# The second mixture reads split rows of tokens from DRAM, with three more places for weight pairs

## The chip, the cores and the metric

One core of a Trainium2 chip runs one program: attention, a mixture of experts with hard routing, and a second mixture with soft weights. The metric is the device time of one execution in microseconds (us). The kernel before takes 2384.46 us, the median of three runs (2382.55 to 2384.86). TensorE (PE in the profile) multiplies, VectorE (DVE), ScalarE (ACT) and GpSimd (POOL) do elementwise work, and SyncE (SP) issues most DMAs, in the order of its program.

## The reference, cut to what matters

The second mixture, for 2304 tokens of width 512, eight experts and a hidden width of 1024:

```python
def _moe2_ref(x, w_gate, w1, w2):
    logits = x @ w_gate
    P = np.exp(logits - logits.max())
    for _ in range(8):
        P /= P.sum(1, keepdims=True) + 1e-09
        P /= P.sum(0, keepdims=True) + 1e-09
        P *= N / E
    out = np.zeros((N, D))
    for e in range(E):
        h = np.maximum(x @ w1[e], 0.0)
        out += P[:, e:e + 1] * (h @ w2[e])
```

Its x is the output of the first mixture, whose own x is the output of attention.

## The kernel before, in words

A float32 product is made of three matmuls: each operand is split into a high part (h at the end of its name: xh, w1h, w2h, hh) and the rest (xl, w1l, w2l, hl), and `mm3` (L842 and after) adds high times high, high times low and low times high. A split costs one copy on ScalarE, which makes the high part, and one subtraction on VectorE or GpSimd, which makes the low one.

The second mixture starts at about 765 us of the profiled execution. It runs over 8 experts, 9 blocks of 256 tokens and 4 steps each: 288 steps of 45 matmuls. In a step, `first` multiplies a block of x by a quarter of w1 (24 matmuls into the PSUM tile ph); then ScalarE makes z (with relu), VectorE four sums of its parts, ScalarE hh and VectorE hl. While that goes on TensorE makes the products of hh, hl of the step before with a quarter of w2 (`second`, 21 matmuls): seven products of Strassen's scheme in place of eight, which is why z has sums and w2 has sums too. `gather_up` adds the products from the PSUM banks (rows u, c) and adds them, times P, to acc.

x stands in SBUF as the tile xT2, unsplit. `split_x` splits a quarter of a block at a time, during the block ahead: two quarters with the subtraction on GpSimd, two on VectorE. Every block is split anew for every expert, 72 times.

The weights of an expert are four w1 pairs and four w2 pairs (a pair is a high and a low tile). They come as raw halves by DMA (`w_load`, 256 KB each, on SyncE), are split by `split`, and for w2 `strassen` also makes sums on GpSimd, in place in raw, between two stages of splits (a third tile, w3, holds two of the seven operands). There are four places for w1 pairs and four for w2 pairs, so the next expert's pair can only be made when the last block of this expert has used the place. `work(2)`, at the end of each step, puts up to two pieces of that into the engines' queues if a place is free. Around each of the seven changes of expert (a boundary below) the four w1 pairs and four w2 pairs of the next expert are made in some seven steps:

```python
if g >= gone[n] + 4 or budget < 1:
    continue
```

Each engine works strictly in the order of its program, which is written by hand from the first mixture on (`manual_schedule`): z and hl of a step stand on VectorE behind the weight splits that the step before put there. In the same way a DMA that waits on SyncE holds up those behind it.

In the first mixture (535 to 765 us) an expert has 288 tokens and 8 steps; xT2 is written at the end of each expert. In the last expert's steps 4 to 7 block 0 is split for the second mixture.

Of the kernel before, what the change touches and what calls it, by code (L numbers as in the profile page):

```python
# [9 lines left out]
F32 = mybir.dt.float32  # L10
# [5 lines left out]
OP = mybir.AluOpType  # L16
# [23 lines left out]
GBUSY = (10, 2, 4)  # L40
FAST = tuple(x.split() for x in (
# [25 lines left out]
def fused_kernel(ctx, tc, qT, kT, vv, wg1, w1a, w2a, wg2, w1b, w2b, out):  # L67
# [11 lines left out]


# [27 lines left out]
    def w_tiles(name, pool=None):  # L108
        pool, k = pool or wpool, {"w1": 4, "w2": 5, "w3": 2}[name]
        return [pool.tile([128, k, 256], F32R, name=name + x, tag=name + x, bufs=NFC // 2) for x in "hl"]  # L110
# [11 lines left out]
    def strassen(t, t2, b1, b2):  # L122
# [3 lines left out]
        seq = [lambda o=o, x=x, y=y: G.tensor_tensor(out=o, in0=x, in1=y, op=OP.subtract)  # L126
                for o, x, y in ((b11, b12, b11), (b12, b22, b12), (b22, b22, b11), (b21, b22, b21))]
# [711 lines left out]
    xT2 = x2.tile([128, NDC, N], F32, name="xT2")  # L839
# [9 lines left out]

    rw = ctx.enter_context(tc.tile_pool(name="rw", bufs=1))  # L850
# [22 lines left out]
    def work(budget):  # L873
# [46 lines left out]
    part1 = ctx.enter_context(ExitStack())  # L920
# [63 lines left out]
    pend, done, xa = None, 0, []  # L984
    for e in range(E):
        x, nxt = nxt, []
        for f in range(NFC):
# [17 lines left out]
            if e == E - 1 and f >= 4:  # L1005
                xa.append(split_x(0, f - 4, V))
# [53 lines left out]
    def first(w1, x, between):  # L1060
# [5 lines left out]
        between()  # L1066
# [4 lines left out]
        A.activation(z[:, :4], ph.rearrange("p f (t n) -> p (f t) n", t=2), AF.Relu)  # L1071
# [182 lines left out]
```

## Time and profile before

| | |
|---|---|
| median of 3 runs | 2384.46 us (2382.55 to 2384.86) |
| profiled execution | 2386.12 us |
| its span, first to last instruction | 2384.2 us |
| TensorE busy in the span | 2283.8 us, 96% |
| VectorE, ScalarE, GpSimd busy | 73%, 53%, 36% |
| granted TensorE clock, mean | 0.983 |
| DMA of SyncE's queue (q1) | 86.66 MB, 12.0% of 16 engines |
| xl on GpSimd, 144 rows | 137.1 us |

A matmul's own time in the profile (0.28 us for 256 columns) overlaps those of its neighbours, so the number of matmuls that pass in a stretch says more of TensorE than its busy time.

### The profile page before, as it was taken

What the parts mean: (1) busy time and instruction counts of PE and PEld (TensorE: products, weight loads), DVE (VectorE), ACT (ScalarE), POOL (GpSimd) and SP (SyncE); (2) the same over time, 40 slices, a digit from 0 to 9 for tenths busy, and PEclk for the clock granted to TensorE, in tenths of its full rate; (3) what the DMA queues carried; (4) which work ended last, traced back from release to release, by engine and by line L of the source; (5) the groups of instructions that cost most, each with busy time, mean ns of one, the idle gap of its engine ahead of it and who ended that gap; (6) DMA issues with size and microseconds to landing.
All of it is one profiled execution on the core that took longest, in us unless ns stands there. A gap on an engine that the chain in (4) does not pass through costs nothing.

```text
span 2384.2 us, 49700 instructions
## 1 busy us (share of the span) xinstructions
PE 2283.8 (96%) x19592; PEld 2158.1 (91%) x19592; DVE 1751.6 (73%) x4432; ACT 1269.8 (53%) x2805; POOL 851.3 (36%) x936
## 2 busy tenths in 40 slices
PE   9999999959999999999899999989999998998998
PEld 6888888729999999899899989989989998998998
DVE  8999999863444776866866786686687668668766
ACT  8999999614555434444444444454444444435443
POOL 6888888504445201400510330050041023005112
PEclk9999999859999999999999999999999999999999
DMA  2102010125554000200200010020010001001000
GB/s 79 56 29 64 26 57 15 36 79 150 169 167 134 28 1 10 63 1 1 63 10 1 28 45 1 1 72 1 1 54 19 1 19 54 1 1 45 23 23 36
DMA packets 54723, 99.36 MB, mean 42 GB/s; under 512 B 10832, under 2 KB 11088, under 8 KB 54480
## 3 DMA queue, kind: packets, MB, share of 16 engines
q1 hardware_dynamic: 51504, 86.66, 12.0%
q0 software_dynamic: 2976, 9.44, 1.1%
q8 instruction: 155, 2.54, 0.4%
q14 instruction: 88, 0.72, 0.1%
HBM read 86.63 MB, written 9.45 MB: 40 GB/s over the span
## 4 chain that ended last, share of the span: by engine, by line
PE 58%; issue 7%; DVE 6%; POOL 4%; ACT 2%; DMA 0%; POOLq 0%; DVEq 0%
PE bank L845 10%; PE bank L847 10%; PE bank L846 10%; PE ph L846 9%; PE ph L845 9%; PE ph L847 9%; POOL raw L126 2%; DVE w2l L115 1%; POOL w1l L115 1%; DVE z L1073 1%; ACT hh L1077 1%; DVE hl L1079 1%; POOL xl L959 1%; PE bank L949 1%; DVE z L1075 1%
## 5 line engine op out<-in xcount | busy, mean ns | idle before, releaser
L845 PE MATMUL ph<-xh,w1h 128*128 128x256 f32 x2304 | 647.2, 281 | 15.8 <-ACT z L1071 15.4
L846 PE MATMUL ph<-xl,w1h 128*128 128x256 f32 x2304 | 646.7, 281 | 9.3 <-DVE xl L959 9.3
L847 PE MATMUL ph<-xh,w1l 128*128 128x256 f32 x2304 | 643.9, 279 | 0.0
L959 POOL TENSOR_TENSOR xl<-xT,xh 128x256 fp32r<-128x256 f32 x144 | 137.1, 952 | 1056.6 <-ACT xh L957 1056.6
L845 PEld LDWEIGHTS ph<-xh,w1h 128*128 128x128 f32 x2304 | 433.3, 188 | 21.4 <-ACT z L1071 21.4
L1071 ACT ACTIVATE z<-ph 128x512 f32<-128x512 f32 x288 | 171.5, 595 | 513.3 <-PE ph L847 507.6
L846 PEld LDWEIGHTS ph<-xl,w1h 128*128 128x128 f32 x2304 | 432.5, 188 | 13.6 <-DVE xl L959 13.6
L847 PEld LDWEIGHTS ph<-xh,w1l 128*128 128x128 f32 x2304 | 432.7, 188 | 0.0
L847 PE MATMUL bank<-w2h,hl 128*128 128x256 f32 x1440 | 408.1, 283 | 14.4 <-DVE hl L1078 14.4
L845 PE MATMUL bank<-w2h,hh 128*128 128x256 f32 x1440 | 405.9, 282 | 10.1 <-ACT c L1099 10.1
L846 PE MATMUL bank<-w2l,hh 128*128 128x256 f32 x1440 | 403.0, 280 | 0.0
L1073 DVE TENSOR_TENSOR z<-z 128x128 f32<-128x128 f32 x288 | 104.3, 362 | 319.8 <-ACT z L1071 319.7
L1077 ACT ACTIVATE hh<-z 128x512 fp32r<-128x512 f32 x288 | 182.2, 633 | 275.0 <-DVE z L1076 275.0
L847 PEld LDWEIGHTS bank<-w2h,hl 128*128 128x128 f32 x1440 | 271.5, 189 | 18.8 <-DVE hl L1078 18.5
L845 PEld LDWEIGHTS bank<-w2h,hh 128*128 128x128 f32 x1440 | 271.0, 188 | 11.5 <-ACT c L1099 11.5
L846 PEld LDWEIGHTS bank<-w2l,hh 128*128 128x128 f32 x1440 | 271.4, 189 | 0.0
L1079 DVE TENSOR_TENSOR hl<-z,hh 128x512 fp32r<-128x512 f32 x288 | 204.4, 710 | 65.8 <-ACT hh L1077 65.8
L267 POOL TENSOR_TENSOR W<-W,sg 128x288 f32<-128x288 f32 x288 | 208.2, 733 | 69.8 <-ACT sg L262 69.2
L115 POOL TENSOR_TENSOR w1l<-raw,w1h 128x512 fp32r<-128x512 f32 x92 | 129.3, 1420 | 173.2 <-ACT w1h L114 147.1
L252 DVE MAX8 upper<-W 128x8 f32<-128x288 f32 x432 | 183.3, 448 | 5.7 <-POOL W L267 4.3
L334 PEld LDWEIGHTS pO<-vt,aT 128*128 128x128 f32 x1280 | 159.3, 193 | 28.2 <-issue 26.3
L291 POOL TENSOR_TENSOR dbuf<-S,upper 128x576 f32<-128x576 f32 x144 | 165.1, 1147 | 0.0
(238 smaller groups left out, 5402.8 us busy)
## 6 DMA issues: line engine op xcount, KB each, us to landing
raw<-in_w1a_dram SPq DMA_DIRECT2D x64, 256.0 KB, 2.9
raw<-in_w2a_dram SPq DMA_DIRECT2D x64, 256.0 KB, 2.8
raw<-in_w2b_dram SPq DMA_DIRECT2D x64, 256.0 KB, 2.7
raw<-in_w1b_dram SPq DMA_DIRECT2D x64, 256.0 KB, 2.6
vt<-in_vv_dram SPq DMA_DIRECT2D x16, 325.0 KB, 3.1
kt<-in_kT_dram SPq DMA_DIRECT2D x16, 288.0 KB, 3.4
qt<-in_qT_dram SPq DMA_DIRECT2D x16, 288.0 KB, 3.7
x_dram<-x SPq DMA_DIRECT2D x15, 256.0 KB, 2.7
```

The lines of the kernel that those rows point to most:

```text
L115: lambda: eng.tensor_tensor(out=t[1][:, s], in0=raw, in1=t[0][:, s], op=OP.subtract)]
L252: V.max(out=upper[:, ST[n]["at"], 8 * k:8 * k + 8], in_=ST[n]["W"])
L267: G.tensor_tensor(out=d["W"], in0=d["W"], in1=d["sg"], op=OP.mult)
L291: G.tensor_tensor(out=flat(d["D"])[:, :S], in0=flat(d["S"]), in1=upper[:, d["at"], 0:1].to_broadcast([128, S]), op=OP.subtract)
L334: PE.matmul(pO[:, 0], aT[:, c, :], vt[:, c, j], start=(c == 0), stop=(c == 4))
L845: PE.matmul(dst, a[0], b[0], start=start, stop=False, **kw)
L846: PE.matmul(dst, a[0], b[1], start=False, stop=False, **kw)
L847: PE.matmul(dst, a[1], b[0], start=False, stop=stop, **kw)
L959: eng.tensor_tensor(out=lo, in0=src, in1=hi, op=OP.subtract)
L1071: A.activation(z[:, :4], ph.rearrange("p f (t n) -> p (f t) n", t=2), AF.Relu)
L1077: A.activation(hh[:, 3:], z[:, 4:], AF.Copy)
L1079: V.tensor_tensor(out=hl[:, 3:], in0=z[:, 4:], in1=hh[:, 3:], op=OP.subtract)
```

## The change

The low and high parts of x are made once for each block and kept in DRAM. Blocks 0 to 6 are split at the ends of the first mixture's experts 1 to 7, as soon as their tokens are there; each is then written by two stores of 512 KB from SyncE (`split_x`). Blocks 7 and 8 are split in steps 0 and 1 of the second mixture. `load_x` reads a block back by two loads; blocks 0 and 1 are loaded at the end of the first mixture, and from then on the last step of each block issues the loads of the block after the next, into two buffers. xT2 is given up after step 3, acc takes room that it had, and after step 6 there are two further places for w1 pairs and one for w2 pairs, used from the second expert on. The sums of z are made in another order and with other signs, and so are those of w2.

```diff
+EXTRA = {"w1": 2, "w2": 1}
+    xp_dram = [[dram.tile([128, NDC * 256], F32, name=f"xp{x}{k}") for x in "hl"] for k in range(N // 256)]
-        seq = [lambda o=o, x=x, y=y: G.tensor_tensor(out=o, in0=x, in1=y, op=OP.subtract)
-                for o, x, y in ((b11, b12, b11), (b12, b22, b12), (b22, b22, b11), (b21, b22, b21))]
+        seq = [lambda o=o, x=x, y=y, op=op: G.tensor_tensor(out=o, in0=x, in1=y, op=op)
+                for o, x, y, op in ((b11, b12, b11, OP.subtract), (b12, b22, b12, OP.subtract),
+                                    (b22, b11, b22, OP.subtract), (b21, b21, b22, OP.add))]
...
+    def places(n, g):
+        return NFC // 2 + (EXTRA[n] if g >= 36 else 0)
+
     def make(n, g, raws):
-        W[n, g] = t = w_tiles(n)
+        at = (more[n], EXTRA[n]) if g >= 36 and (g - 36) % places(n, g) < EXTRA[n] else ()
+        W[n, g] = t = w_tiles(n, *at)
...
-            if g >= gone[n] + 4 or budget < 1:
+            if g >= gone[n] + places(n, g) or budget < 1 or g >= 36 and not more:
                 continue
...
-    def split_x(blk, d, eng):
+    def split_x(t, blk, d):
 
         src = xT2[:, d, blk * 256:(blk + 1) * 256]
-        hi = xs.tile([128, 256], F32R, name="xh", bufs=6)
-        A.activation(hi, src, AF.Copy)
-        lo = xs.tile([128, 256], F32R, name="xl", bufs=6)
-        eng.tensor_tensor(out=lo, in0=src, in1=hi, op=OP.subtract)
-        return hi, lo
+        A.activation(t[0][:, d], src, AF.Copy)
+        V.tensor_tensor(out=t[1][:, d], in0=src, in1=t[0][:, d], op=OP.subtract)
+        if d == NDC - 1:
+            for k in range(2):
+                nc.sync.dma_start(xp_dram[blk][k], all_of(t[k]).bitcast(F32))
+
+    def load_x(blk):
+        t = x_tiles(xs, 2)
+        for k in range(2):
+            nc.sync.dma_start(all_of(t[k]).bitcast(F32), xp_dram[blk][k])
+        return [(t[0][:, d], t[1][:, d]) for d in range(NDC)]
...
-            if e == E - 1 and f >= 4:
-                xa.append(split_x(0, f - 4, V))
+            if f >= 4 and (halved + (f > 4)) * 256 < e * CAP and (f > 4 or (halved + 1) * 256 <= e * CAP):
+                if f == 4:
+                    xt = x_tiles(xs, 2)
+                split_x(xt, halved, f - 4)
+                halved += f == NFC - 1
+            if e == E - 1 and f == NFC - 1:
+                xa = [load_x(0), load_x(1)]
...
-        V.tensor_tensor(out=z[:, 4], in0=z[:, 0], in1=z[:, 2], op=OP.add)
-        V.tensor_tensor(out=z[:, 6], in0=z[:, 1], in1=z[:, 0], op=OP.subtract)
-        V.tensor_tensor(out=z[:, 5], in0=z[:, 4], in1=z[:, 1], op=OP.subtract)
-        V.tensor_tensor(out=z[:, 7], in0=z[:, 3], in1=z[:, 5], op=OP.subtract)
+        sums(4, 2, 0, OP.add)
+        sums(5, 1, 4, OP.subtract)
+        sums(7, 3, 5, OP.add)
+        sums(6, 1, 0, OP.subtract)
...
-                both("u3", "u3", p4, OP.subtract, to=(t1, l)), *put("u3", t1, l), *scale(t1), *store(t1)]
+                both("u3", "u3", p4, to=(t1, l)), *put("u3", t1, l), *scale(t1), *store(t1)]
...
-            h = first(need("w1", 32 + 4 * e + i), x,
-                      lambda: xa.extend(split_x((blk + 1) % nb, d, V) for d in (2, 3)) if i == 3 else None)
+            h = first(need("w1", 32 + 4 * e + i), x)
+            if i == 3 and eb + 2 < E * nb:
+                xa.append(load_x((blk + 2) % nb))
...
-        if i == 1 or i == 2:
-            xa.append(split_x((blk + 1) % nb, i - 1, G))
+        if s < nb - halved:
+
+            xt = x_tiles(sx, 2)
+            for d in range(NDC):
+                split_x(xt, halved + s, d)
+        if s == 3:
+            turned.close()
+            ac = late["ac"] = ctx.enter_context(tc.tile_pool(name="ac", bufs=1))
+            late["acc"] = ac.tile([128, NT, D], F32, name="acc")
+        if s == 6:
+            more["w1"] = ctx.enter_context(tc.tile_pool(name="w1x", bufs=1))
+            more["w2"] = ctx.enter_context(tc.tile_pool(name="w2x", bufs=1))
```

VectorE's order at the change from the second to the third expert, last block, third step. Before: the second stage of one w2 pair (w2l, w3l), the first stage of the next (w2l, w2l), two rows of x, then the sums z and the two hl of the following step.

```order
L115 TENSOR_TENSOR w2l<-raw,w2h 128x512
L115 TENSOR_TENSOR w3l<-raw,w3h 128x512
L115 TENSOR_TENSOR w2l<-raw,w2h 128x256
L115 TENSOR_TENSOR w2l<-raw,w2h 128x512
L959 TENSOR_TENSOR xl<-xT_19437,xh 128x256 x2
L1073 TENSOR_TENSOR z<-z 128x128
L1074 TENSOR_TENSOR z<-z 128x128
L1075 TENSOR_TENSOR z<-z 128x128
L1076 TENSOR_TENSOR z<-z 128x128
L1078 TENSOR_TENSOR hl<-z,hh 128x384
L1079 TENSOR_TENSOR hl<-z,hh 128x512
```

The same place on VectorE in the changed kernel:

```order
L118 TENSOR_TENSOR w2l<-raw,w2h 128x512
L118 TENSOR_TENSOR w3l<-raw,w3h 128x512
L118 TENSOR_TENSOR w2l<-raw,w2h 128x256
L118 TENSOR_TENSOR w2l<-raw,w2h 128x512
L1102 TENSOR_TENSOR z<-z 128x128 x4
L1111 TENSOR_TENSOR hl<-z,hh 128x384
L1112 TENSOR_TENSOR hl<-z,hh 128x512
```

The two rows of x are gone; the splits of the weights stand where they stood.

One step on, VectorE before: the end of the last block's fourth step and the next expert's first step.

```order
L115 TENSOR_TENSOR w2l<-raw,w2h 128x512
L115 TENSOR_TENSOR w3l<-raw,w3h 128x512
L1073 TENSOR_TENSOR z<-z 128x128
L1074 TENSOR_TENSOR z<-z 128x128
L1075 TENSOR_TENSOR z<-z 128x128
L1076 TENSOR_TENSOR z<-z 128x128
L1078 TENSOR_TENSOR hl<-z,hh 128x384
L1079 TENSOR_TENSOR hl<-z,hh 128x512
L1108 TENSOR_TENSOR u_27386<-bank_19458,c_27384 128x256
L1108 TENSOR_TENSOR u_27388<-bank_19459,u_27386 128x256
L115 TENSOR_TENSOR w2l<-raw,w2h 128x256
L115 TENSOR_TENSOR w2l<-raw,w2h 128x512
```

The same place on VectorE in the changed kernel:

```order
L118 TENSOR_TENSOR w2l<-raw,w2h 128x512
L118 TENSOR_TENSOR w3l<-raw,w3h 128x512
L118 TENSOR_TENSOR w2l<-raw,w2h 128x256
L118 TENSOR_TENSOR w2l<-raw,w2h 128x512
L1102 TENSOR_TENSOR z<-z 128x128 x4
L1111 TENSOR_TENSOR hl<-z,hh 128x384
L1112 TENSOR_TENSOR hl<-z,hh 128x512
L1141 TENSOR_TENSOR u_27344<-bank_19475,c_27342 128x256
L1141 TENSOR_TENSOR u_27346<-bank_19476,u_27344 128x256
L118 TENSOR_TENSOR w2l<-raw,w2h 128x512
L118 TENSOR_TENSOR w3l<-raw,w3h 128x512
```

The third pair's first stage stands a step earlier and its second stage follows a step earlier too; the fourth pair comes where it came.

SyncE's order at the start of the second mixture, before: only raw halves of weights.

```order
L105 DMA raw<-in_w2b_dram 128x512 x2
L105 DMA raw<-in_w1b_dram 128x512 x2
L105 DMA raw<-in_w2b_dram 128x512 x2
L105 DMA raw<-in_w1b_dram 128x512 x4
L105 DMA raw<-in_w2b_dram 128x512 x4
```

The same place on SyncE in the changed kernel (xph, xpl: the DRAM tiles of a block's high and low part):

```order
L108 DMA raw<-in_w1b_dram 128x512 x2
L108 DMA raw<-in_w2b_dram 128x512 x2
L978 DMA xph_80<-xh 128x1024
L978 DMA xpl_81<-xl 128x1024
L983 DMA xh<-xph_68 128x1024
L983 DMA xl<-xpl_69 128x1024
L983 DMA xh<-xph_70 128x1024
L983 DMA xl<-xpl_71 128x1024
L108 DMA raw<-in_w1b_dram 128x512 x2
```

The loads of blocks 0 and 1 stand behind the stores of block 6, and raw halves behind all six.

## Rows read from the trace of the kernel before

**Rows 1.** Busy time by stretch, quiet and boundary: PE, PEld, DVE, ACT, POOL, clock, DMA, GB/s.

```profile
900.00:948.00 48.00, 48.00 (x410) 48.00 (x409) 29.78 (x81) 20.30 (x40) 4.09 (x5) 1.00 0.00 1
1151.05:1199.47 48.42, 41.09 (x325) 38.84 (x323) 46.19 (x82) 25.59 (x53) 28.26 (x26) 1.00 0.31 87
```

**Rows 2.** Waits of PE from 790 us: who for whom, total, times, longest.

```profile
PE ph L845 <- ACT z L1071: 15.4, 20, 1.1
PE bank L847 <- DVE hl L1078: 14.4, 20, 1.0
PE bank L845 <- ACT c L1099: 10.1, 7, 1.7
PE ph L846 <- DVE xl L959: 9.3, 21, 1.1
```

**Rows 3.** DVE by line, 1151.05 to 1199.47: count, busy us, mean ns, idle before.

```profile
L115 DVE TENSOR_TENSOR w2l<-raw,w2h 128x512 fp32r<-128x512 f32 (+1 forms) x12 | 11.2, 961 | 0.0
L115 DVE TENSOR_TENSOR w3l<-raw,w3h 128x512 fp32r<-128x512 f32 x4 | 3.8, 958 | 0.0
L959 DVE TENSOR_TENSOR xl<-xT,xh 128x256 fp32r<-128x256 f32 x4 | 2.6, 677 | 0.0
```

**Rows 4.** POOL by line in the same stretch.

```profile
L126 POOL TENSOR_TENSOR raw<-raw 128x256 f32<-128x256 f32 x16 | 15.2, 949 | 5.1 <-DVE w2l L115 4.1
L115 POOL TENSOR_TENSOR w1l<-raw,w1h 128x512 fp32r<-128x512 f32 x6 | 9.2, 1554 | 7.0 <-ACT w1h L114 7.0
L959 POOL TENSOR_TENSOR xl<-xT,xh 128x256 fp32r<-128x256 f32 x4 | 4.0, 1002 | 2.3 <-ACT xh L957 2.3
```

**Rows 5.** Instructions in order of time, same boundary: start us, us, engine, line.

```profile
1151.26 0.28 DVE L1074 TENSOR_TENSOR z<-z 128x128 f32<-128x128 f32 x1
1151.46 0.29 DVE L1075 TENSOR_TENSOR z<-z 128x128 f32<-128x128 f32 x1
1151.78 0.29 DVE L1076 TENSOR_TENSOR z<-z 128x128 f32<-128x128 f32 x1
...
1161.50 1.16 POOL L959 TENSOR_TENSOR xl<-xT,xh 128x256 fp32r<-128x256 f32 x1
1161.98 0.41 DVE L1108 TENSOR_TENSOR c<-c,bank 128x256 f32<-128x256 f32 x1
...
1163.19 0.68 DVE L115 TENSOR_TENSOR w2l<-raw,w2h 128x512 fp32r<-128x512 f32 x1
...
1171.47 1.48 POOL L115 TENSOR_TENSOR w1l<-raw,w1h 128x512 fp32r<-128x512 f32 x1 [2.78 <-ACT w1h L114]
1171.72 1.78 DVE L115 TENSOR_TENSOR w2l<-raw,w2h 128x512 fp32r<-128x512 f32 x1
```

**Rows 6.** Instructions in order of time where the second mixture starts.

```profile
764.32 0.41 ACT L957 ACTIVATE xh<-xT 128x256 fp32r<-128x256 f32 x1
...
765.07 0.28 PE L845 MATMUL ph<-xh,w1h 128*128 128x256 f32 x1
...
765.14 0.42 DVE L959 TENSOR_TENSOR xl<-xT,xh 128x256 fp32r<-128x256 f32 x1
```

**Rows 7.** DMA issues of raw halves: count, KB each, median us to landing.

```profile
raw<-in_w1b_dram SPq DMA_DIRECT2D x64, 256.0 KB, 2.6
```

**Rows 8.** Busy time by stretch, first mixture's end, start, steps 6 to 9, slow clock.

```profile
700.00:765.00 65.00, 65.00 (x503) 65.00 (x502) 29.06 (x55) 33.65 (x77) 32.63 (x28) 1.00 0.50 143
765.00:790.00 25.00, 25.00 (x199) 24.82 (x198) 18.15 (x35) 13.66 (x31) 14.46 (x14) 0.93 0.26 75
801.80:823.50 21.70, 21.70 (x186) 21.70 (x185) 16.51 (x51) 8.73 (x19) 1.88 (x2) 1.00 0.00 1
967.00:970.40 3.40, 3.40 (x18) 3.40 (x18) 3.14 (x7) 1.66 (x4) 1.15 (x2) 0.51 0.00 0
```

**Rows 9.** Instructions in order of time, first mixture: a w1 pair's raw halves and their use.

```profile
739.61 1.56 SPq L105 DMA_DIRECT2D raw<-in_w1b_dram  x2
...
745.20 1.15 ACT L114 ACTIVATE w1h<-raw 128x512 fp32r<-128x512 f32 x2
```

More of the change, by code (lines that the diff above doesn't have):

```diff
@@ L106, in w_load, with w_tiles @@
         return raw
-    def w_tiles(name, pool=None):
+    def w_tiles(name, pool=None, bufs=NFC // 2):
         pool, k = pool or wpool, {"w1": 4, "w2": 5, "w3": 2}[name]
-        return [pool.tile([128, k, 256], F32R, name=name + x, tag=name + x, bufs=NFC // 2) for x in "hl"]
+        return [pool.tile([128, k, 256], F32R, name=name + x, tag=name + x, bufs=bufs) for x in "hl"]
     def split(t, s, raw, eng):
@@ L838, in fused_kernel @@
     x2 = ctx.enter_context(tc.tile_pool(name="x2", bufs=1))
-    xT2 = x2.tile([128, NDC, N], F32, name="xT2")
     L2 = x2.tile([128, NT, E], F32, name="L2")
@@ L855, in fused_kernel @@
     turns = [0]
+    more = {}
+    def places(n, g):
+        return NFC // 2 + (EXTRA[n] if g >= 36 else 0)
     def make(n, g, raws):
-        W[n, g] = t = w_tiles(n)
+        at = (more[n], EXTRA[n]) if g >= 36 and (g - 36) % places(n, g) < EXTRA[n] else ()
+        W[n, g] = t = w_tiles(n, *at)
         if n == "w2" and g >= 32:
-            W["w3", g] = w_tiles("w3", w3)
+            W["w3", g] = w_tiles("w3", *(at or (w3,)))
             return strassen(t, W["w3", g], *raws)
@@ L917, in half_bank @@
         return bank[k // 2][:, k % 2]
-    part1 = ctx.enter_context(ExitStack())
+    turned = ctx.enter_context(ExitStack())
+    xT2 = turned.enter_context(tc.tile_pool(name="xt", bufs=1)).tile([128, NDC, N], F32, name="xT2")
+    part1 = turned.enter_context(ExitStack())
     xg_p = part1.enter_context(tc.tile_pool(name="xg_p", bufs=1))
@@ L951, in logits2, with x_tiles, all_of @@
         A.activation(L2[:, t0:t1].rearrange("p t e -> p (t e)"), pl[:, :(t1 - t0) * E], AF.Copy)
-    def split_x(blk, d, eng):
-        src = xT2[:, d, blk * 256:(blk + 1) * 256]
-        hi = xs.tile([128, 256], F32R, name="xh", bufs=6)
-        A.activation(hi, src, AF.Copy)
-        lo = xs.tile([128, 256], F32R, name="xl", bufs=6)
-        eng.tensor_tensor(out=lo, in0=src, in1=hi, op=OP.subtract)
-        return hi, lo
+    def x_tiles(pool, bufs):
+        return [pool.tile([128, NDC, 256], F32R, name="x" + x, tag="x" + x, bufs=bufs) for x in "hl"]
+    def all_of(t):
+        return t.rearrange("p d n -> p (d n)")
+    def split_x(t, blk, d):
+        src = xT2[:, d, blk * 256:(blk + 1) * 256]
+        A.activation(t[0][:, d], src, AF.Copy)
[8 more added lines that the diff above has]
+        return [(t[0][:, d], t[1][:, d]) for d in range(NDC)]
     def second1(e, f, h):
@@ L983, in fused_kernel @@
         f()
-    pend, done, xa = None, 0, []
+    pend, done, xa, halved, xt = None, 0, [], 0, None
     for e in range(E):
@@ L1058, in fused_kernel, with first @@
     sink = [(logits_end, max_a), (max_t, max_b)] + [(lambda pm: None, rows), (sums_t, columns)] * 8
-    def first(w1, x, between):
+    def first(w1, x):
         ph = ps.tile([128, 2, 256], F32, name="ph")
@@ L1065, in first @@
                 mm3(ph[:, f], cols(w1, f, d), x[d], d == 0, d == NDC - 1, skip_group_check=True)
-        between()
         z = xs.tile([128, 8, 128], F32, name="z")
@@ L1069, in first, with sums @@
         hl = xs.tile([128, 7, 128], F32R, name="hl", bufs=2)
-        A.activation(z[:, :4], ph.rearrange("p f (t n) -> p (f t) n", t=2), AF.Relu)
+        q = ph.rearrange("p f (t n) -> p (f t) n", t=2)
+        def sums(o, x, y, op):
+            V.tensor_tensor(out=z[:, o], in0=z[:, x], in1=z[:, y], op=op)
+        A.activation(z[:, :4], q, AF.Relu)
         A.activation(hh[:, :3], z[:, 1:4], AF.Copy)
-        V.tensor_tensor(out=z[:, 4], in0=z[:, 0], in1=z[:, 2], op=OP.add)
-        V.tensor_tensor(out=z[:, 6], in0=z[:, 1], in1=z[:, 0], op=OP.subtract)
-        V.tensor_tensor(out=z[:, 5], in0=z[:, 4], in1=z[:, 1], op=OP.subtract)
-        V.tensor_tensor(out=z[:, 7], in0=z[:, 3], in1=z[:, 5], op=OP.subtract)
+        sums(4, 2, 0, OP.add)
+        sums(5, 1, 4, OP.subtract)
+        sums(7, 3, 5, OP.add)
+        sums(6, 1, 0, OP.subtract)
         A.activation(hh[:, 3:], z[:, 4:], AF.Copy)
@@ L1186, in fused_kernel @@
             part1.close()
-            ac = late["ac"] = ctx.enter_context(tc.tile_pool(name="ac", bufs=1))
-            late["acc"] = ac.tile([128, NT, D], F32, name="acc")
+            sx = turned.enter_context(tc.tile_pool(name="sx", bufs=1))
         else:
```

2 lines of the change are left out of this document (1 added, 1 removed).

## The prediction

> **What bounds the kernel now.** I read the busy time by stretch first. In a quiet stretch of the second mixture TensorE is busy all the time and passes 410 matmuls in 48 us, 0.117 us each; VectorE is busy 29.78 us of it [rows 1]. A stretch of 48.42 us around a change of experts passes only 325 matmuls, 38.0 us of work: 10.4 us are lost there. There are seven such stretches, so about 72.5 us in all. In them it is VectorE that has no room: 46.19 us busy of 48.42 [rows 1].
>
> Second, who makes TensorE wait: four results, and none of them is a weight half. They are z (15.4 us, 20 times), hl (14.4, 20 times), the copy c (10.1, 7 times) and xl (9.3, 21 times, three a boundary) [rows 2]. z, hl and c come from ScalarE or VectorE and stand in their queues behind the splitting of the next expert's weights. So weights aren't late; making them in one burst delays other things.
>
> Third, what VectorE does there. The 16 split rows of four w2 pairs take 11.2 + 3.8 us and four xl rows 2.6 us [rows 3]; GpSimd is busy 28.26 us with w1l, the in-place subtractions on raw, and four xl (4.0 us) [rows 4]. The two hinder each other: a 512-wide w2l takes 0.68 us alone and 1.78 us beside a w1l of GpSimd, while a VectorE row that reads a PSUM bank takes 0.41 us beside an xl of GpSimd [rows 5]. How much in all: quiet work for 325 matmuls is 29.78 x 325/410 = 23.6 us, and 12 splits at 0.68 with 4 at about 0.42 are 9.9 us; 33.5 us together against 46.19, so 12.7 us are lost to 28.26 us of GpSimd, 0.45 us for each.
>
> **The change part by part.**
>
> *Three more places.* They let the first w2 pair and the first two w1 pairs of an expert be built long before its boundary. But a place that comes free is filled at once, so at six of the seven boundaries as many pairs are still built as before: the order of VectorE has the four w2 pairs in the same six steps, the third one even a step earlier. Later deadlines take away a wait on weights, and rows 2 has none. I cost this at 0 for six boundaries. At the last boundary nothing follows: one w2 pair (9.9/4 = 2.5 us of VectorE) and, on GpSimd, a quarter of the raw rows (3.8 us) and two of three w1 pairs counted there (6.1 us) are gone, 9.9 x 0.45 = 4.5 us.
>
> *Split rows not made 72 times.* The three waits for xl at a boundary go [rows 2]; what is late next are hl and z. At each boundary 2.6 us of VectorE [rows 3] and 4.0 us of GpSimd [rows 4] go. The second is worth between 0 and 4.0 us; by the ratio 1.8; but beside reads of PSUM it costs nothing, so I count half of it, 0.9. In quiet steps TensorE waits for none of this: nothing is gained there.
>
> *The new order of the sums.* Before, one z row follows at once on the one it reads: starts 0.32 us apart instead of 0.20 [rows 5]. Now two do. That is up to 0.12 us in each of the 7 steps of a boundary, 0.8 us, or nothing where GpSimd sets the pace; I take 0.5. The changed signs leave the same number of rows of the same shapes.
>
> Per boundary: 2.6 + 0.9 - 0.5 = 3.0 us, six times 18.0. The last: 3.0 + 2.5 + 4.5 = 10.0; three pairs still stand in consecutive steps there, so I take 8.0. Together -26.0 us (bounds: 1.8 x 6 + 5 = 16 and 6.1 x 6 + 10.4 = 47).
>
> *The start of the second mixture.* Here the change adds a wait. Before, TensorE starts its first step at 765.07, and the last xl ends at 765.14 + 0.42 = 765.56 [rows 6], in time for the matmuls that need it. Now that last split is followed on SyncE's one queue by two stores of block 6, then the loads of block 0 and block 1. A 512 KB transfer at 143/0.50 = 286 GB/s [rows 8] takes 1.83 us; 256 KB land 2.6 us after issue [rows 7], so 1.7 us are fixed. If the loads run beside the stores, block 0 is there at 765.56 + 1.7 + 1.83 = 769.1; if the four go one behind the other, at 765.56 + 1.7 + 4 x 1.83 = 774.6. TensorE's queue holds only matmuls behind that first one, so it idles 4 to 9.5 us; I take 7.5, near the serial end, since one queue issues all four. The Trainium skill, "DMA: Bandwidth & Descriptors", section "Queues, rings and completion order", says that descriptors of one issuing engine are consumed in ring order on each DMA engine; by that rule alone the idle time would be the serial 9.5 us and the forecast 2371 us. No run here shows it yet.
>
> In 3.4 us after the first stalls of the first boundary TensorE's granted clock is 0.51, the lower of its two levels (1.2 GHz instead of 2.4), and 18 matmuls pass instead of 29 [rows 8], 1.3 us lost. After the new idle time it may do the same: 0 to 1.7 us, I take 0.9. Blocks 7 and 8 are split whole on VectorE in the first two steps: 8 xl at 0.42 = 3.4 us, 4 of them new work for VectorE and two moved to an earlier step, where VectorE is busy 18.15 of 25 us [rows 8]: 0 to 3.4, I take 1.5. The pairs for the new places are built in steps 6 to 8, where VectorE has 21.7 - 16.51 = 5.2 us free [rows 8] for 2.5 + 4.5 us: 0 to 2, less the xl rows gone there; I take 0.5. The 28 splits at the ends of the first mixture's experts are hidden: before, the last expert does the same four, and TensorE is busy 65.00 of 65.00 us [rows 8]. Without that cover they would cost 28 x 0.42 = 12 us. Loads in the later blocks are issued two blocks, over 21 us, ahead of a need that takes about 1.7 + 2 x 1.83 = 5.4 us: hidden.
>
> Sum: -26.0 + 7.5 + 0.9 + 1.5 + 0.5 = -15.6 us. The profiled execution took 2386.12 us, 1.7 above the median 2384.46 of the runs; from the median the forecast is 2369 us.
>
> **Rivals.**
>
> *The port decides (bigger gain).* If at the boundaries VectorE and GpSimd take turns throughout, each xl of GpSimd gives back its whole length: 2.6 + 4.0 - 0.5 = 6.1 us, six times 36.6, and the last boundary all its 10.4; with the 10.4 us of costs -36.6, or 2348 us. For it: 1.78 against 0.68 us. Against: 0.41 us beside an xl [rows 5]. The Trainium skill, "SBUF — State Buffer", section "SBUF: two separate sides", says that GpSimd and a VectorE row with two SBUF inputs hold a shared port pair exclusively for a whole instruction. By that rule alone it would be this rival; the two rows just named agree with it and also show where it doesn't bite.
>
> *Deadlines decide.* If the stalls came from late weights, all 72.5 us would come back: -72.5 + 10.4 = -62, 2322 us. Against it: no weight in rows 2, and an unchanged burst.
>
> *Only the direct wait goes.* If the queue behind xl is filled by the next late result (hl), the gain is what TensorE waited for xl itself, 9.3 us [rows 2], and the 10.4 us of costs eat it: 2386 us, no change.
>
> *Slower: raw weights queue behind x.* All these transfers share SyncE's queue. In the first mixture the second raw half of a w1 pair is issued at about 740.8, lands near 743.4, and ScalarE wants it at 745.20 [rows 7, 9]: 1.8 us to spare. The two stores of a block (2 x 1.83 = 3.7 us) in front of it make it 1.9 us late, and ScalarE, whose hh rows stand behind, waits in order. From a delay above 1.8 us this decides. Seven stores in the first mixture and seven boundaries where loads of x stand in front of raw: 14 x 1.9 = 27 us, so -15.6 + 27 = +11, 2396 us.
>
> **How the numbers follow.** My forecast has a chance of 0.52, the port 0.14, deadlines 0.05, only the direct wait 0.17, the slower rival 0.12. A measurement here tells a change of about 0.2%, 4.8 us, from none. Faster: nearly all of the first (0.49), port and deadlines (0.19), a little of the fourth (0.04): 0.72. Same: most of the fourth and bits of the others, 0.14. Slower 0.14. The forecast's own range is 2357 to 2380 (small gain with the serial start, large gain with a short one); to hold 8 in 10 it must take in the port and the direct-wait case: 2346 to 2387.
>
> **What would show it.** Right: boundaries of some 350 matmuls in 48.42 us (48.42 - 7.4 = 41.0 us at 0.117), VectorE still near 46 us busy there, TensorE waiting for z, hl and c but not for xl; one idle stretch of TensorE of 5 to 9 us at about 765 us, ended by a DMA of x; quiet stretches unchanged at 0.117 us. Wrong: boundaries without loss (deadlines), raw landings after 745 us followed by ScalarE's waits in the first mixture (the slower rival), or a load of x late in every block.

## The result, and the profile after

The changed kernel takes 2405.53 us (median of 4 runs, 2402.41 to 2410.11), the kernel before beside it 2383.51: ratio 1.0093, 95% interval 1.0075 to 1.011. It is slower by 22 us where 15 us less was forecast. Its profiled execution is the quickest of its four, 2402.41 us with a span of 2400.6 us; the traces explain 16.4 us, the difference of the two spans.

To see where the time went I took the starts of TensorE's 288 steps of the second mixture from both traces. "Loss at the boundaries" is the time of ten steps at each change of expert, two ahead of it and eight behind, less ten quiet steps of 5.3 us, summed over the seven.

| us | before | after | difference |
|---|---|---|---|
| start to end of the first mixture's matmuls, up to the second's first | 765.1 | 773.5 | +8.4 (0.9 of it ahead of the first mixture) |
| steps 0 to 3 | 24.8 | 29.3 | +4.5 |
| steps 4 to 19 | 87.9 | 92.2 | +4.3 |
| loss at the boundaries | 72.6 | 69.5 | -3.1 |
| quiet steps between the boundaries | 901.6 | 903.4 | +1.8 |
| from the last boundary to the end | 161.2 | 161.7 | +0.5 |

The busy time by stretch, one quiet stretch, the same boundary as in [rows 1], and the last boundary (columns as there):

```profile
1120.00:1168.00 48.00, 48.00 (x408) 48.00 (x407) 29.62 (x78) 17.77 (x33) 2.28 (x2) 1.00 0.13 45
1168.00:1216.42 48.42, 41.92 (x331) 40.66 (x330) 46.47 (x80) 23.65 (x46) 23.19 (x23) 0.96 0.38 117
2178.00:2226.42 48.42, 44.31 (x355) 43.50 (x354) 40.95 (x82) 20.44 (x39) 13.80 (x14) 0.96 0.18 61
```

The quiet stretch is as before. The boundary passes 331 matmuls, not 350 (325 before). GpSimd has 5 us less to do there, 23.19 against 28.26, and VectorE still none to spare: 46.47 against 46.19. Only the last boundary, behind which nothing is built, reaches what was forecast for all.

What makes TensorE wait, from 790 us on (total, times, longest; c is the copy out of a PSUM bank, the row L a late one of step 8):

```profile
PE bank L850 <- DVE hl L1111: 34.9, 25, 2.9
PE bank L848 <- ACT c L1132: 8.4, 6, 2.4
PE bank L1077 <- DVE L L1074: 3.2, 2, 2.4
PE ph L848 <- ACT z L1103: 0.3, 1, 0.3
```

Beside [rows 2], xl is gone (9.3 us) and so is z (15.4), but hl went from 14.4 to 34.9 us. The sum of hl, c, z and xl falls by little: 49.2 us before, 43.6 now. The single waits are longer: none above 1.7 us before, up to 2.9 us now. Lines of VectorE and GpSimd in that boundary, to be read beside [rows 3] and [rows 4]:

```profile
L1102 DVE TENSOR_TENSOR z<-z 128x128 f32<-128x128 f32 x30 | 15.2, 526 | 2.4 <-ACT z L1103 1.9
L118 DVE TENSOR_TENSOR w2l<-raw,w2h 128x512 fp32r<-128x512 f32 (+1 forms) x12 | 10.1, 870 | 0.0
L118 DVE TENSOR_TENSOR w3l<-raw,w3h 128x512 fp32r<-128x512 f32 x4 | 3.9, 964 | 0.0
L1111 DVE TENSOR_TENSOR hl<-z,hh 128x384 fp32r<-128x384 f32 x7 | 6.0, 854 | 0.0
```

```profile
L129 POOL TENSOR_TENSOR raw<-raw 128x256 f32<-128x256 f32 x16 | 13.8, 865 | 9.0 <-DVE w2l L118 8.1
L118 POOL TENSOR_TENSOR w1l<-raw,w1h 128x512 fp32r<-128x512 f32 x7 | 10.4, 1507 | 8.6 <-ACT w1h L117 8.6
```

The same 16 weight splits and 16 in-place rows of GpSimd stand in the same boundary: the burst wasn't thinned. The costliest line of VectorE is one that the forecast's rows left out, the sums z, at 526 ns a row. In order of time, one step of that boundary:

```profile
1190.34 2.66 DVE L1102 TENSOR_TENSOR z<-z 128x128 f32<-128x128 f32 x4
1192.92 1.08 DVE L1111 TENSOR_TENSOR hl<-z,hh 128x384 fp32r<-128x384 f32 x1
1193.92 0.68 DVE L1112 TENSOR_TENSOR hl<-z,hh 128x512 fp32r<-128x512 f32 x1
```

```profile
1189.89 3.69 POOL L129 TENSOR_TENSOR raw<-raw 128x256 f32<-128x256 f32 x4 [3.89 <-DVE w2l L118]
```

and the same four sums in a step without GpSimd:

```profile
1168.36 1.15 DVE L1102 TENSOR_TENSOR z<-z 128x128 f32<-128x128 f32 x4 [1.91 <-ACT z L1103]
1169.42 0.55 DVE L1111 TENSOR_TENSOR hl<-z,hh 128x384 fp32r<-128x384 f32 x1
```

Alone 1.15 us, beside the four rows on raw 2.66 us. It was no different in the kernel before; one of its steps, beside four rows on raw from 1188.25 to 1192.35 us:

```profile
1188.70 0.83 DVE L1073 TENSOR_TENSOR z<-z 128x128 f32<-128x128 f32 x1
1189.45 0.28 DVE L1074 TENSOR_TENSOR z<-z 128x128 f32<-128x128 f32 x1
1189.65 0.83 DVE L1075 TENSOR_TENSOR z<-z 128x128 f32<-128x128 f32 x1
1190.51 0.78 DVE L1076 TENSOR_TENSOR z<-z 128x128 f32<-128x128 f32 x1
1191.21 0.55 DVE L1078 TENSOR_TENSOR hl<-z,hh 128x384 fp32r<-128x384 f32 x1
```

The four sums took 2.59 us there, but the first hl behind them 0.55. In the changed kernel, the chain of waits (start us, us, what) shows how:

```profile
1190.42 0.76 DVE z L1102
...
1191.20 0.80 DVE z L1102
...
1192.06 0.66 issue
1192.72 0.29 DVE z L1102
```

Three of the four sums come 0.7 to 0.9 us apart, near the length of one row of GpSimd (3.69 / 4 = 0.92 us), as if one of those got in between each two; the last sum takes 0.29 us. The first hl behind them takes 1.08 instead of 0.55 us.

The second finding is the granted clock. Boundaries of ten steps each, of the seven before the first two, and two of the seven after:

```profile
952.07:1014.81 62.74, 57.05 (x453) 55.18 (x451) 54.97 (x106) 32.13 (x67) 29.95 (x28) 0.97 0.23 62
1152.70:1216.20 63.50, 56.17 (x453) 53.92 (x451) 56.64 (x110) 32.13 (x67) 30.14 (x28) 1.00 0.22 62
```

```profile
1170.04:1232.81 62.77, 56.27 (x452) 55.01 (x451) 55.77 (x104) 28.30 (x55) 22.93 (x22) 0.97 0.31 101
...
1571.89:1637.52 65.63, 59.06 (x452) 57.81 (x451) 55.92 (x104) 28.33 (x55) 22.66 (x22) 0.92 0.30 97
```

Before, one boundary of seven had a clock under 1.00; now all have, 0.97 in six and 0.92 in one. In the trace's own steps of the clock that is one stretch of 3.4 us at 1.2 GHz (half clock) before, and seven such and one of 6.8 us now; the part below full clock, half of that time, was 1.7 us in all and is 15.4 us now. One of the stretches:

```profile
1187.20:1190.60 3.40, 3.40 (x19) 3.40 (x18) 3.36 (x8) 1.76 (x4) 0.71 (x1) 0.50 0.23 68
```

It begins 0.7 us after a wait for hl of 1.9 us. But not every long wait is followed by one: behind the wait of 2.9 us at 1206.4 in the same boundary the clock stayed at 1.00, and the one stretch of before lies in a boundary without a wait above 1.2 us.

Third, the start of the second mixture, to be read beside [rows 6]: busy time by stretch, SyncE's queue, TensorE.

```profile
768.00:770.00 2.00, 0.00 (x0) 0.00 (x0) 0.00 (x0) 0.00 (x0) 0.80 (x1) 1.00 1.05 421
...
772.00:774.00 2.00, 0.47 (x1) 0.29 (x1) 0.00 (x0) 0.00 (x0) 0.00 (x0) 0.50 0.93 324
...
770.80:781.00 10.20, 6.53 (x28) 6.26 (x29) 0.04 (x1) 0.63 (x2) 0.00 (x0) 0.50 0.66 250
```

```profile
766.17 0.42 SPq L978 DMA_DIRECT2D xph<-xh  x1
766.65 0.42 SPq L978 DMA_DIRECT2D xpl<-xl  x1
767.11 0.97 SPq L983 DMA_DIRECT2D xh<-xph  x1
768.12 1.22 SPq L983 DMA_DIRECT2D xl<-xpl  x1
```

```profile
773.52 0.55 PE L848 MATMUL ph<-xh,w1h 128*128 128x256 f32 x1 [7.38 <-issue]
775.03 0.58 PE L849 MATMUL ph<-xl,w1h 128*128 128x256 f32 x1 [0.95 <-DMA xl<-xpl]
```

Two stores and two loads were issued one behind the other, and landed so, at 770.0, 771.5, 773.4 and 775.0 us; xh was there after about 7.4 us of idling, xl 1.5 us later, and then TensorE ran at 1.2 GHz until 781.0 us. The first step took 8.57 us instead of 4.44.

### The profile page after: what moved, and what is told of

Same layout as the page of the kernel before. It is cut to its first block, busy times and chain, and to the rows that moved or that the text cites. A ratio compares the mean times of both kernels' runs of the same rounds, so it can differ in the third digit from the quotient of the medians.

```text
span 2400.6 us, 49352 instructions
## 1 busy us (share of the span) xinstructions
PE 2291.5 (95%) x19592; PEld 2171.9 (90%) x19592; DVE 1727.2 (72%) x4320; ACT 1180.7 (49%) x2549; POOL 704.1 (29%) x792
## 4 chain that ended last, share of the span: by engine, by line
PE 59%; DVE 10%; issue 6%; ACT 2%; POOL 1%; DMA 1%; SPq 0%; POOLq 0%; DVEq 0%; ACTq 0%
PE bank L850 10%; PE bank L848 10%; PE bank L849 10%; PE ph L848 9%; PE ph L849 9%; PE ph L850 9%; DVE z L1102 3%; DVE w2l L118 3%; DVE hl L1112 1%; DVE hl L1111 1%; DVE w3l L118 1%; ACT hh L1110 1%; DVE u L1141 1%; POOL out_dram L1168 0%; PE bank L961 0%
## 5 line engine op out<-in xcount | busy, mean ns | idle before, releaser
L1102 DVE TENSOR_TENSOR z<-z 128x128 f32<-128x128 f32 x1152 | 354.6, 328 | 413.3 <-ACT z L1103 393.6
L850 PE MATMUL bank<-w2h,hl 128*128 128x256 f32 x1440 | 411.7, 286 | 34.9 <-DVE hl L1111 34.9
L1111 DVE TENSOR_TENSOR hl<-z,hh 128x384 fp32r<-128x384 f32 x288 | 174.7, 606 | 0.0
```

Of the source, the lines that this page charges most:

```text
L850: PE.matmul(dst, a[1], b[0], start=False, stop=stop, **kw)
L1102: V.tensor_tensor(out=z[:, o], in0=z[:, x], in1=z[:, y], op=op)
L1111: V.tensor_tensor(out=hl[:, :3], in0=z[:, 1:4], in1=hh[:, :3], op=OP.subtract)
```

## The experiments

Four questions: what each of the four parts of the change costs alone; what makes the boundaries slow; whether the order of the sums is the part that failed, and why; and what the three places are good for. The runs stand on several chips; each ratio is to runs of the kernel before on the same chip. "After" is the changed kernel. "Boundaries" below is the loss defined above, from one trace each, 72.6 us before and 69.5 us after.

**The old order of the sums in the changed kernel.** 6 in front of 5 again:

```diff
         sums(4, 2, 0, OP.add)
+        sums(6, 1, 0, OP.subtract)
         sums(5, 1, 4, OP.subtract)
         sums(7, 3, 5, OP.add)
-        sums(6, 1, 0, OP.subtract)
```

> The changed kernel with the four sums of z in the order of before (z4, z6, z5, z7: only one of them reads the row just ahead of it), the new signs kept. In the changed kernel a boundary passes about 331 matmuls in 48.42 us where 350 were forecast; beside GpSimd the time from the first sum to the second hl is 3.6 us a step, 3.3 before. Theory order (the new order took the gain: each dependent sum waits anew for GpSimd): 0.3 us in five steps of a boundary, 0.1 in the others, and no half-clock stretch behind the shortened stalls: 2 to 3.5 us a boundary, 14 to 25 us in all, so 2378 to 2391 us where the changed kernel takes about 2402 to 2405. Theory places (the burst stands otherwise on the engines): 0 to 4 us, 2399 to 2405 us.

2397.69 us, ratio 1.005 (1.0037 to 1.0063): 8 us less than after. Boundaries 64.2. The sign is right, the size under what was expected. The same step as above:

```profile
1192.46 2.57 DVE L1102 TENSOR_TENSOR z<-z 128x128 f32<-128x128 f32 x4
1194.95 0.55 DVE L1111 TENSOR_TENSOR hl<-z,hh 128x384 fp32r<-128x384 f32 x1
1195.73 0.91 DVE L1112 TENSOR_TENSOR hl<-z,hh 128x512 fp32r<-128x512 f32 x1 [0.23 <-ACT hh L1110]
```

The sums take no less, but the first hl takes 0.55 instead of 1.08 us and the second 0.91 instead of 0.68: the first ends 3.04 us after the first sum starts (3.66 in the new order), the second 4.18 (4.26). TensorE's waits for hl fall from 34.9 to 21.7 us. The clock does not come back, though: it is 0.94 to 0.97 in six boundaries, and the part below full clock is 17.1 us where it was 15.4.

**The new order alone, in the kernel before.** L1074 (z6) moved behind z7.

> The kernel before with the new order of the sums alone (z4, z5, z7, z6). Theory order: the boundaries get longer by 2 to 3.5 us each, 14 to 25 us in all, 2398 to 2409 us, and the granted clock falls at each boundary as it does in the changed kernel. Theory places: 0.12 us more in seven steps of a boundary, under 6 us in all, 2384 to 2390 us.

2392.60 us, ratio 1.0034 (1.0022 to 1.0047): slower by 8 us, between the two expectations. Boundaries 81.7, +9.1. Its waits:

```profile
PE bank L847 <- DVE hl L1078: 27.8, 24, 2.3
PE bank L845 <- ACT c L1099: 10.8, 7, 1.7
```

With xl (7.8), z (4.4) and 0.9 of a fifth line that is 51.7 us, 1.7 more than the same five before, but gathered in hl, up to 2.3 us at a time where hl took 1.0 at most; and the clock is 0.97 in all seven boundaries, 11.9 us below full clock where it was 1.7. By this count most of the 9.1 us lies in the clock, not in more waiting.

**No further places.** `EXTRA = {"w1": 0, "w2": 0}` in the changed kernel, and no pools for them.

> The changed kernel without the three places: four for w1 pairs and four for w2 pairs as before, x from DRAM and the new order kept. Theory places: the third w2 pair stands a step later again, GpSimd's raw rows stand beside the sums in four steps of a boundary instead of five, and the 4.1 us lost in step 8 come back: boundaries pass 340 to 350 matmuls in 48.42 us, 15 to 25 us less than the changed kernel, 2378 to 2390 us. Theory order: only the 4.1 us of step 8 and perhaps 1 us a boundary, 2391 to 2400 us.

2401.71 us, ratio 1.0074 (1.0061 to 1.0087), 4 to 5 us under after, less than the spread of after's own runs. Neither expectation. Boundaries 72.0: the last one loses 9.8 us where it loses 6.9 with the places, the other six together 62.2 and 62.5. Steps 4 to 19 at 88.0 instead of 92.2, quiet steps at 901.6 instead of 903.4: what the places give at the last boundary they take back elsewhere.

**Block 0 loaded early.** The last expert's end splits nothing (block 6 is split in steps 0 to 2 with 7 and 8), and the loads of blocks 0 and 1 are issued seven steps earlier:

```diff
-            if f >= 4 and (halved + (f > 4)) * 256 < e * CAP and (f > 4 or (halved + 1) * 256 <= e * CAP):
+            if e < E - 1 and f >= 4 and (halved + (f > 4)) * 256 < e * CAP and (f > 4 or (halved + 1) * 256 <= e * CAP):
...
-            if e == E - 1 and f == NFC - 1:
+            if e == E - 1 and f == 0:
```

> The changed kernel with blocks 0 and 1 loaded at the start of the first mixture's last expert, some 27 us ahead of their use, and block 6 split in the second mixture's first three steps with blocks 7 and 8 (not at the end of the first mixture). This measures the start alone: TensorE's idle 9.6 us at 766 to 775 us go, and the half clock behind it (10.2 us at 0.5, of which some 3 us count). Both theories: 9 to 13 us less than the changed kernel, 2390 to 2395 us; less gain, down to 6 us, if the third block's four splits on VectorE in step 2 delay the sums there.

2398.49 us, ratio 1.0058 (1.0045 to 1.0071): 7 us back, less than the 9 to 13 expected. The idle stretch is gone; the first mixture up to the second's first step gains 5.8 us on after (7.6 but for its first products, which ran at half clock in this trace), steps 0 to 3 gain 2.6. Boundaries 72.7, 3.2 more than after, though this run changes nothing there; two of them have a clock of 0.92. So 3 us of this figure between two traces say nothing by themselves.

**All three together: early load, no places, old order.** What is left of the change is x from DRAM (and the signs of the sums, with the same rows).

> The changed kernel with blocks 0 and 1 loaded early, no further places, and the old order of the sums: what is left of the change is x from DRAM. If the three costs add up (start about 10 us by the run with the early load, order 5 to 9 us by the stretches of the two runs on it, places 3 to 4 us), it takes 2379 to 2386 us, and its seven boundaries lose 62 to 68 us together against 72.6 before: x from DRAM is worth 1 us a boundary. If x from DRAM is worth the 3.5 us a boundary of the forecast, the boundaries lose 48 us and it takes about 2362 us.

2373.40 us, ratio 0.9956 (0.9942 to 0.9969): faster than before, between the expectations. Boundaries 57.4, though four of them have a clock of 0.97. TensorE reaches its first step of the second mixture 224.2 us after its first of the first mixture, as before.

**The same with the new order.** One edit between this run and the last.

> The run with early load, no places and old order, but with the new order of the sums: one edit apart from it (2373.4 us, boundaries 57.4 us). By the stretches of the run without places (72.0 us, new order) the order is worth 2 us a boundary here: boundaries 70 to 74 us and 2386 to 2391 us, which would make up for all that x from DRAM gains. Rival: the 72.0 came of the late load and not of the order: boundaries 58 to 62 us, 2374 to 2378 us.

2389.86 us, ratio 1.0018 (1.0009 to 1.0027), as the theory of the order expected: by the two ratios these four lines cost 15 us (16.5 by the two medians, which are of different chips). Boundaries 71.5, +14.1. Main waits of this kernel, and of the one with the old order:

```profile
PE bank L850 <- DVE hl L1111: 37.4, 26, 2.3
PE bank L848 <- ACT c L1132: 10.7, 7, 1.9
```

```profile
PE bank L850 <- DVE hl L1111: 16.0, 17, 1.5
PE ph L848 <- ACT z L1103: 11.5, 15, 2.2
PE bank L848 <- ACT c L1132: 10.5, 6, 1.7
```

Over the boundary steps in which the four sums took more than 1.3 us (29 in each kernel), the four sums take 2.66 us in both. But the first hl ends 3.64 us after the first sum starts in the new order and 3.13 in the old, the second 4.48 and 4.26; in quiet steps the first ends after 1.63 and 1.50. So the order costs 0.13 us where VectorE is alone, which is what the forecast had, and 0.5 us beside GpSimd: 29 x 0.51 = 14.8 us, about what the boundaries lose, though the two need not be the same microseconds. In the new order the first hl takes over 0.8 us in 28 of the 29 steps, in the old one in none; there it is the second hl in 28 (12 in the new), which TensorE needs later.

The rows show where the slow ones fall. With the old order, in most of these steps (20 of 29 here, 21 of 21 in the kernel with one stage a step, below), the rows z4, z6, z5, z7, first hl, second hl are slow, fast, slow, slow, fast, slow (a sum 0.7 to 0.8 us or 0.28, the first hl 1.08 or 0.55, the second 0.9 or 0.68); with the new one (16 of 29, and 21 of 21), z4, z5, z7, z6, first hl, second hl are slow, slow, slow, fast, slow, fast. Four are slow in either; a row that does not read the result of the slow row just ahead is the fast one. The old order gave that place behind z7 to the first hl, the new one gives it to z6. That is read from durations; no run tests it by itself.

**GpSimd's sums of w2 left out**, to see what the boundaries cost without them.

```diff
-        return [split(t, slice(0, 1), b1[:, 0:1], V) + split(t, slice(1, 3), b2, V), seq,
+        return [split(t, slice(0, 1), b1[:, 0:1], V) + split(t, slice(1, 3), b2, V), [],
```

> The changed kernel without the four in-place sums of w2 that GpSimd makes for each pair (left out, so the products of the second mixture are of other operands; VectorE's and ScalarE's rows stay the same). At a boundary 13.8 of GpSimd's 23 to 24 us go. Theory contention (VectorE's sums wait for GpSimd's rows, which makes the steps of a boundary long): z takes 1.0 us for four rows beside nothing instead of 2.7, five steps a boundary, so the boundaries lose some 2 to 4 us each instead of 9.9, 40 to 55 us less in all, 2350 to 2365 us. Theory backlog (VectorE has too many rows of its own there: 15 us of splits): the boundaries still lose 7 us or more each, 2385 us or more.

2341.42 us, ratio 0.982 (0.9805 to 0.9836), more than either theory had. Boundaries 14.7, though VectorE has the same splits to make; the wait for hl is 6.7 us in all, 0.9 at most, and the clock is 1.00 in all seven. The sums take what they take alone:

```profile
1173.99 1.14 DVE L1102 TENSOR_TENSOR z<-z 128x128 f32<-128x128 f32 x4
1175.05 0.55 DVE L1111 TENSOR_TENSOR hl<-z,hh 128x384 fp32r<-128x384 f32 x1
```

So it isn't the number of rows on VectorE that makes the boundaries late, but their meeting with the 256-wide rows of GpSimd. (Of the 59 us between the two traces 54.8 are at the boundaries.)

**The far pairs later.** With early load and old order, the places are used to put off work: one piece a step in the middle of an expert, and no pair of an expert whose turn is not near.

```diff
-            if g >= gone[n] + places(n, g) or budget < 1 or g >= 36 and not more:
+            if g >= gone[n] + places(n, g) or budget < 1 or g >= 36 and not more or g // 4 - 8 > last:
...
-        work(2)
+        work(1 if 1 < blk < nb - 1 else 2, e + (blk >= (2 if e else 5)))
```

> The changed kernel with the early load, the old order, and one rule more: a pair for the expert after the next is only built from the third block of an expert on (in the first expert from the sixth), one piece a step. The places stay. So the first six boundaries carry what the last one does, two w1 pairs and three w2 pairs in six steps. If places help once the burst isn't refilled, each boundary loses 5 to 7 us, as the last one does in the changed kernel and with the old order (6.9, 5.1), 35 to 49 us in all instead of 69.5; with the start (10 us) and the order, 2355 to 2370 us. If the burst isn't what counts, the boundaries stay near 9.5 us and it takes 2385 to 2390 us.

2360.91 us, ratio 0.9899 (0.9883 to 0.9914), as expected. Boundaries 41.7.

**And at most one stage of a w2 pair in a step**, so that two stages with their GpSimd rows no longer stand in one:

```diff
+            if n == "w2" and g >= 36:
+                if one:
+                    continue
+                one.append(g)
```

> As the run with far pairs later, and at most one stage of a w2 pair in a step: the three pairs of a boundary stand in six steps, two splits in each, no step with four. That uses the later deadlines. Theory burst (VectorE has about 2 us free in each step, and a stall comes where a step gets more than that): a boundary loses 0 to 3 us, 2330 to 2350 us. Rival (each z beside GpSimd's raw rows is late by itself): 4 to 6 us a boundary stay, 2355 to 2370 us.

2327.65 us, ratio 0.9765 (0.9751 to 0.9778): the best of all, 2.3% under the kernel before and a little better than expected. Boundaries 7.5. The longest line of TensorE's waits (the others come to 1.5 us), and one boundary of ten steps:

```profile
PE bank L848 <- ACT c L1136: 4.6, 6, 0.8
```

```profile
1147.10:1201.32 54.22, 53.46 (x452) 53.26 (x451) 45.98 (x100) 24.71 (x47) 14.51 (x14) 1.00 0.27 86
```

The four sums still take 2.6 us where they meet GpSimd, but in only three of a boundary's steps (21 in all seven boundaries, 29 before), with steps free of it in between. No run has this limit without the three places, so what the limit alone would give isn't shown.

**The new order in that kernel.**

> The run with one piece a step, but with the new order of the sums. Theory: the order costs where each dependent sum and the first hl behind them wait for a row of GpSimd and VectorE has no room left; in a spread burst it has room, so 0 to 3 us more than the 2328 us of that run. Rival: the order costs the same 1.3 to 2.1 us a boundary however the burst stands, 9 to 15 us more, 2337 to 2343 us.

2334.41 us, ratio 0.9788 (0.9775 to 0.9802). That is 5 to 7 us above the old order (by the ratios and by the medians, which are of different chips) and 3.7 us at the boundaries by the traces, between the two expectations: the order costs less where the burst is thin, but I can't call it free.

**The first hl ahead of the sums**, since that is what TensorE waits for:

```diff
+        V.tensor_tensor(out=hl[:, :3], in0=z[:, 1:4], in1=hh[:, :3], op=OP.subtract)
+
         sums(4, 2, 0, OP.add)
...
-        V.tensor_tensor(out=hl[:, :3], in0=z[:, 1:4], in1=hh[:, :3], op=OP.subtract)
```

> The changed kernel with the first hl row (384 wide, the one that TensorE needs first) ahead of the four sums instead of behind them; the second hl and ScalarE's second hh come later for it, by about 0.55 us a step. Theory: what the new order makes late is this first hl (it ends 0.6 us later beside GpSimd), and TensorE waits for it 34.9 us in all; with it ahead that wait falls below 10 us and the boundaries lose 5 to 15 us less, 2388 to 2398 us if the chip's other parts stay. Rival: VectorE's queue as a whole is late, so the wait only moves to the copy c, z or the second hl, and the time stays within 4 us of the changed kernel's 2402 to 2406.

2437.77 us, ratio 1.0219 (1.0205 to 1.0233): slower by 30 to 32 us than after, against the theory. Boundaries 95.9.

```profile
PE bank L848 <- ACT hh L1111: 26.0, 20, 2.1
PE bank L848 <- ACT c L1132: 22.5, 7, 3.5
PE bank L850 <- DVE hl L1112: 8.4, 22, 0.8
```

The first hl is no longer late (1.7 us in another line), but the second hh is, which ScalarE makes from the four sums, and with it c, which stands behind it on ScalarE. VectorE now also idles for the first hh ahead of that row, and the sums all come later. So "TensorE waits for the first hl" is too narrow: sums, hh and both hl are one chain, and whatever is put behind in it becomes the late one. Of the orders run here, the old one is the one in which none stood out.

## Why the prediction was wrong

Each row below differs from the row above by one part; the times are set against the kernel before on the same chip.

| kernel | us | against before beside it | boundaries | the part |
|---|---|---|---|---|
| before | 2384 | | 72.6 | |
| x from DRAM, loaded early, no places, old order | 2373.4 | -10.9 | 57.4 | x from DRAM: -10.9 |
| the same, new order | 2389.9 | +4.6 | 71.5 | order of the sums: +15.5 |
| the same, block 0 loaded late | 2401.7 | +17.2 | 72.0 | start: +12.6 |
| after (with the places) | 2405.5 | +22.0 | 69.5 | places: +4.8 (within the spread of the runs) |

The parts depend on what stands beside them: in after itself the old order gives back 8 us and the early load 7. At the boundaries -26.0 us were forecast and -3.1 measured; that is 23 of the 32 us between the forecast of -15.6 and the traces' +16.4.

*The step that failed* is "Per boundary: 2.6 + 0.9 - 0.5 = 3.0 us", in its last term above all. That term, the new order, was sized at the wrong place. I took 0.12 us a step from [rows 5], from sums that ran while GpSimd was idle, and wrote "nothing where GpSimd sets the pace". It is the other way round: alone the order costs 0.13 us a step, as forecast, and beside GpSimd about 0.5. The term was 3.5 us for the seven boundaries (0 to 0.8 us each); it measured 14.1 us there in the changed kernel without places, 9.1 us in the kernel before and 5.3 us in the changed kernel as it stands. That the four sums take 2.6 us beside rows on raw stood in the trace of before; I read them in a step without.

*x from DRAM at the boundaries*: 2.6 + 0.9 = 3.5 us each was forecast, 24.5 us in seven; 15.2 us were measured, 2.2 us each. The mechanism held in part (xl isn't waited for any more, VectorE and GpSimd have fewer rows), the size was too large: the time of the removed rows was counted in full, but only the wait for xl, 9.3 us, went. TensorE still waits 38.0 us for hl, z and c with x from DRAM and the old order, where it waited 39.9 before. What else makes up the 15.2 us is open.

*Three more places*: 0 at six boundaries was right (together they lose 62.5 us with them, 62.2 without; the order of VectorE showed it). The last boundary, 10.4 us before and 6.9 after, gained 3.5 of the 8.0 forecast. The cost of building pairs early was taken as 0.5 us and measured 4.2: step 8, where they are built, took 9.62 us instead of 5.56; with the work held back, in the best kernel, it takes 5.56 again. With the old order the boundaries lose even more with the places and the late load (64.2) than without either (57.4), which the runs don't take apart further.

*The start*: 7.5 + 0.9 + 1.5 = 9.9 us forecast, 7.6 + 4.5 = 12.1 us measured in the trace, 7 us by loading early in the changed kernel and 13 us by loading late in the one without places. The traces have 10.2 us in both of these pairs: 7.6 up to the first step (half clock at the first mixture's first products, which came and went between runs, left out) and 2.6 in steps 0 to 3. The mechanism was right and its range too: the idle time was 7.4 us and then 0.9 us more for xl, 8.3 us in all, near the serial end. The Trainium skill, "DMA: Bandwidth & Descriptors", section "Queues, rings and completion order", by which descriptors of one issuing engine are consumed in ring order on each DMA engine, agrees: two stores and two loads landed 1.5 to 1.9 us apart in the order of their issue, at 324 to 421 GB/s in the stretches shown. The clock was under-sized: 10.2 us at 0.50, where I had counted 0 to 1.7 us lost.

*The clock at the boundaries* was in no term. The forecast took each boundary's stalls as they were; the clock fell to 0.97 and less in every boundary, where it had been 1.00 in six of seven. The new order alone does that to the kernel before, but it isn't the only thing that does: with the old order the clock is below 1.00 in six boundaries of the changed kernel and in four with early load and no places. Waits and clock can't simply be added to the loss: they give 59.0 of 69.5 us in after, but 50.9 of 72.6 in before, the rest being in matmuls that the view shows as busy. How much of the 14.1 us is clock therefore stays open; between the two kernels that differ in the order alone the sum of waits differs by 12.4 us and the part below full clock by 3.4.

*The rivals.* "The port decides" had the cause right: VectorE's rows meeting GpSimd's make the boundary (14.7 us without the w2 sums, against 69.5). But it counted only on the x rows; those that hurt are the rows on raw, and they stayed. The Trainium skill, "SBUF — State Buffer", section "SBUF: two separate sides", by which the two engines hold the shared ports for a whole instruction, agrees with the 0.7 to 0.8 us from sum to sum, where they take about 0.3 us alone. "Deadlines decide" fell as it was put (the places alone give 2.9 us, at the last boundary), yet with the places and the limits on what stands in a step the work is put off and thinned, and then nearly all of the loss comes back. "Only the direct wait goes" was nearest for x: the wait for xl went and the others stayed (38.0 against 39.9 us), and the 15.2 us lie between its 9.3 and the forecast's 24.5; the long wait for hl came with the order, not out of the queue behind xl, and what it took as cost was too small. "Raw weights queue behind x" fell: TensorE has no idle time in the first mixture, up to its end, in any run, and with the stores of blocks 0 to 5 and block 0 loaded early it takes 224.2 to 226.6 us where it took 224.2, the difference lying in its first products, ahead of any store. No rival had the time: the slower side came from the sums' order, which stood in my sum as a small cost.

*What I asked to see*: no wait for xl at the boundaries, VectorE near 46 us busy, one idle stretch at the start ended by a load of x (the view says "issue", but xh landed at 773.4 us and TensorE went on at 773.5), quiet steps unchanged: all seen. Some 350 matmuls at the boundaries: 331, seen only at the last (355). Behind the start no load of x was waited for; they are issued one block ahead (21 us), not two as the prediction has it.

## What to carry to other kernels

Price a reordering of short rows in a stretch where another engine's rows get in between, not where they run alone: it can put such a row in front of the very result that is wanted first. Further buffers that are refilled at once don't thin a burst; here they paid once the refill was also put off and limited to one stage in a step (2373 to 2328 us, the limits and the places together). When two waits vanish and a third grows by as much, look at the longest single wait and at the granted clock, not at the sum alone.

## What the runs showed of the hardware

- Four 128-wide sums on VectorE took 1.02 us alone in the old order and 1.15 in the new; beside four 256-wide rows of GpSimd they took 2.57 to 2.66 us in either order. Three of the four took 0.7 to 0.8 us there and one 0.28, the one that does not read the result of the slow row just ahead (in 21 of 21 steps in two kernels, 20 and 16 of 29 in two others).
- Stalls of TensorE up to 0.9 us left the granted clock at 1.00 at all boundaries (the kernel with one stage in a step, the one without the w2 sums). Of the longer ones, some were followed by 3.4 to 6.8 us at 1.2 GHz and some not: in one boundary of the changed kernel a stall of 1.9 us was and one of 2.9 us wasn't. In the kernel before, c was waited for up to 1.7 us, and six boundaries of seven stayed at 1.00.
- After the idle time at the start of the second mixture TensorE was at 1.2 GHz for 10.2 us, from 770.8 to 781.0, the first 2.7 us of them idle.
